# The opening of a fused Fourier and feed-forward kernel: loading the first batch's x chunk by chunk, a third fold buffer, and the first weights issued ahead of a store

## The chip, the cores and the metric

The kernel runs on one NeuronCore of a Trainium2 chip. The metric is device time in microseconds (us) of one execution; less is better. The engines are TensorE (PE), VectorE (DVE), ScalarE (ACT), GpSimd (POOL) and SyncE (SP). SP, ACT and POOL issue the DMAs.

## The reference, cut to what matters

```python
def _attn_ref(x):                       # x: 8 x 3008 x 256
    X = np.fft.fft(x, axis=1)
    X = np.fft.fft(X, axis=2)
    return X.real.astype(np.float32)

def _moe_ref(x, w_in, w_out):           # 24064 x 256, 256 x 2048, 2048 x 256
    h = x @ w_in
    g = h * np.cos(h)
    return (g @ w_out).astype(np.float32)
```

The rows of the first function's result, 8 x 3008 of them, are the tokens of the second.

## The kernel before, in words

**The work.** The sequence transform is split as 3008 = 47 x 64. Its first half (47 points) is a set of matmuls over folded x, its second half (64 points) a set of matmuls with the table `BJ`. The transform along the 256 columns is not done on x at all: it is multiplied into the first weights (`weights`, `keep_weights`: the table `CS` times a 512-column piece of `moe_w_in` gives a piece of `WC` and of `WS`). After that the program is a list of 8 batches x 6 groups x 8 steps, two half steps each, in which PE multiplies (`mm1`, L676, and `mm2`, L767), ACT, DVE and POOL form h * cos(h) between the two, and the groups' results are stored. The transform of batch b + 1 is spread over the steps of batch b. Batch 0 has nothing in front of it, so its transform is an opening of its own, ahead of the first step. The change touches this opening alone.

**The opening.** Batch 0 is loaded as eight chunks of four columns i of x, in the order `parts = (2, 3, 4, 5, 0, 1, 6, 7)`; two neighbouring chunks share one x tile (`xp`). A chunk is four DMAs of `load_x`: direct rows 0 to 31 (128 KB) and 32 to 46 (64 KB) from SP's queue, and the mirrored rows (128 KB and 64 KB, the same rows read backwards in i, in runs of 1 KB) from the queue `other`. For each chunk, `fold` then adds and subtracts columns on DVE (two instructions, L299) and copies two columns on POOL (L306); `first_half` multiplies the folded tile `xf` on PE (L320 to L335) into the PSUM tile `pz`; and ACT copies that to `zs` (L346). Fold tiles come from the pool tag "S" with 3 buffers, of which the opening uses two, by the parity of the chunk number. A fold into a buffer waits until PE has read what stood there.

**The z path.** `store_z(p, 0, 4)` writes the first four of 24 output columns of a pair of chunks (pair p holds chunks 2p and 2p + 1) to a DRAM tile `zd`; `load_z` reads them back transposed as `z`; `second_half(0, 0)` multiplies them with `BJ` into `pb` (L507), from which ACT makes `pq`, the first operand of the steps.

**The weights' path.** `load_cs` loads `CS` (256 KB), `load_w(q)` the q-th piece of `moe_w_in` (512 KB). `weights` is the PE work at L583.

**What sets the order.** The order of instructions on each engine is written out by hand, there is no scheduler. SP executes its DMA issues in program order, waits included. Before: eight issues for chunks 2 and 3 (SP and ACT four each), then `load_x(parts[2], 2, nc.scalar)`, one call of four DMAs for chunks 4 and 5 together, then within the loop the direct rows of chunks 0, 1, 6 and 7 from SP and their mirrored rows from POOL, issued by POOL after its copies of the chunk in hand. Row 32 (`load_row`, L164) goes over POOL too. After the loop: `store_z(1)`, `store_z(2)`, `load_cs`, `load_w(0)`, `store_z(0)` on SP.

**The semaphores of the DMAs.** The DMAs of SP and ACT share eight completion semaphores, taken in turn. An issue that takes a semaphore again waits until the DMA that had it has landed. So at most eight DMAs of these two engines are under way.

**Keeping PE busy.** `keep_busy` issues matmuls on constants (L622) ahead of chunk 2 and behind chunks 2 and 3.

Of the kernel before, what the change touches and what calls it, by code (L numbers as in the profile page):

```python
# [11 lines left out]
FP = mybir.dt.float32  # L12
# [11 lines left out]
IP = 4  # L24
# [105 lines left out]
def kernel(  # L130
# [7 lines left out]
    nc = tc.nc  # L138
# [12 lines left out]
    spool = ctx.enter_context(tc.tile_pool(name="work", bufs=1))  # L151
# [10 lines left out]
    def load_row():  # L162
        for r0, r1, at, by in ((0, 32, 1, 3), (31, 47, 5, 6)):
            nc.gpsimd.dma_start(out=xs[0, 0][at:NX:by, 0:ND], in_=x_r[0, r0:r1, 32, :])  # L164

    def load_x(c, m, other):
        p, q = divmod(c, 2)
        xv = xs[0, p].rearrange("r (i d) -> r i d", d=ND)
        i0, k0 = IP * c, IP * q
        k1 = k0 + IP * m  # L170
        i1 = i0 + IP * m
        skip = 1 if c == 0 else 0
        for r0, r1, at, by in ((0, 32, 0, 3), (31, 47, 2, 6)):
            lo, hi = xv[at:NX:by], xv[at + by // 2 : NX : by]
            nc.sync.dma_start(out=lo[:, k0:k1], in_=x_r[0, r0:r1, i0:i1, :])
            other.dma_start(
                out=hi[:, k0 + skip : k1], in_=x_r[0, r0:r1, 64 - i0 - skip : 64 - i1 : -1, :]
            )
# [55 lines left out]
    def load_cs(eng):  # L234
        eng.dma_start(
            out=CS.rearrange("p (i d) -> p i d", i=2),
            in_=CS_dr.ap().rearrange("(i p) d -> p i d", p=128),
        )

    def load_w(q, eng=nc.sync, i0=0, i1=2):  # L240
        eng.dma_start(
            out=wr[q][:, 512 * i0 : 512 * i1].rearrange("p (i f) -> p i f", f=512),
            in_=moe_w_in[128 * i0 : 128 * i1, 512 * q : 512 * q + 512].rearrange(
                "(i p) f -> p i f", p=128
            ),
        )
# [15 lines left out]
        take_x(0, p)  # L262
    parts = (2, 3, 4, 5, 0, 1, 6, 7)
    for c in parts[:2]:
        load_x(c, 1, nc.scalar)
    WC = cpool.tile([128, NDFF], FP, tag="WC", name="WC")
    WS = cpool.tile([128, NDFF], FP, tag="WS", name="WS")
    wn = cpool.tile([128, 16], FP, tag="wn", name="wn")
# [20 lines left out]
        small.clear()  # L289

    xfs = {}
    xf0 = [spool.tile([128, 2 * IP * 128], FP, tag="S", bufs=3, name="xf") for _ in range(2)]

    def fold(c, e, eng=nc.vector):
        lo = IP * (c % 2)
        xv = xs[0, c // 2].rearrange("r (i d) -> r i d", d=ND)[0:NX, lo : lo + IP]
        xfs[c] = xf0[c % 2]
        fv = xfs[c].rearrange("r (e i d) -> r e i d", e=2, d=128)[0:NX]
        eng.tensor_tensor(  # L299
            out=fv[:, e, :, 1:128],  # L300
            in0=xv[:, :, 1:128],
            in1=xv[:, :, 255:128:-1],
            op=ALU.subtract if e else ALU.add,
        )
        if e:
            nc.gpsimd.tensor_copy(  # L306
                out=fv[:, :, :, 0].rearrange("r e i -> r i e"), in_=xv[:, :, 0:129:128]
            )


    def first_half(c):

        fv = xfs.pop(c).rearrange("r (e c) -> r e c", e=2)[0:NX]
        LE, LO, LE0, LO0, LM = (L[0:NX, 64 * q : 64 * q + 64] for q in range(5))
        pz = psum("pz", "M")
        a = 128 if c == 0 else 0
        for e, (w, w0) in enumerate(((LE, LE0), (LO, LO0))):
            rows = slice(64 * e, 64 * e + 64)
            if a:
                nc.tensor.matmul(  # L320
                    pz[rows, 0:128], lhsT=w0, rhs=fv[:, e, 0:128], start=True, stop=True
                )
            nc.tensor.matmul(
                pz[rows, a:512],
                lhsT=w,
                rhs=fv[:, e, a:512],
                start=not a,
                stop=True,
                skip_group_check=True,
            )  # L330
        if a:
            nc.tensor.matmul(
                pz[64:128, 0:1], lhsT=LE0, rhs=fv[:, 1, 0:1], start=True, stop=True
            )
        nc.tensor.matmul(  # L335
            pz[64:128, a:512:128],
            lhsT=LM,
            rhs=fv[:, 1, a:512:128],
            start=True,
            stop=True,  # L340
        )
        p, q = divmod(c, 2)
        if q == 0:
            tag, n, m = ("xp", 4, XP * ND) if p in (0, 3) else ("zs", 2, 1024)
            zps[p] = spool.tile([128, m], FP, tag=tag, bufs=n, name="zs")
        nc.scalar.copy(out=zps[p][:, 512 * q : 512 * q + 512], in_=pz)  # L346
# [105 lines left out]
    def take_zd(b, half):  # L452
        if (b, half) not in zds:
            zds[b, half] = dpool.tile([32, 2 * NJ * 128], FP, tag="zd", bufs=4, name="zd")
        return zds[b, half]

    def store_z(p, j0=0, j1=NJ, engs=(nc.sync, nc.sync)):
        half, q = divmod(p, 2)
        zd, zs = take_zd(0, half), zps[p][:, 0:1024]
        for e in range(2):  # L460
            p0 = 16 * e + XP * q
            engs[e].dma_start(
                out=zd[p0 : p0 + XP, 256 * j0 : 256 * j1].rearrange("i (y d) -> y i d", d=128),
                in_=zs[64 * e + 2 * j0 : 64 * e + 2 * j1, :].rearrange("y (i d) -> y i d", d=128),
            )
# [155 lines left out]
    def keep_busy(pd, n, start):  # L621
        nc.tensor.matmul(  # L622
            pd[:, 0:n],
            lhsT=VX[:, 0:128],
            rhs=VX[:, 0:n],
            start=start,
            stop=True,
            skip_group_check=True,
        )
# [281 lines left out]
    pds = [psum("pd", tag) for tag in ("H", "H", "M")]  # L911
    for pd in pds:
        keep_busy(pd, 512, True)
    load_x(parts[2], 2, nc.scalar)
    for k, c in enumerate(parts):
        for e in range(2):
            fold(c, e)
        if k == 1:
            load_row()
        if 1 <= k < 5:  # L920
            load_x(parts[3 + k], 1, nc.gpsimd)
        first_half(c)
        for _ in range((1, 2)[k] if k < 2 else 0):
            keep_busy(pds[0], 256, False)
    store_z(1, 0, 4)
    store_z(2, 0, 4)
    load_cs(nc.sync)
    load_w(0)
    store_z(0, 0, 4)
    load_w(1, nc.gpsimd)  # L930
    store_z(3, 0, 4, (nc.sync, nc.scalar))
# [186 lines left out]
```

## Time and profile before

| what | value |
|---|---|
| device time, three runs | 1925.84, 1927.04, 1927.95 us (median 1927.04) |
| profiled execution: device time | 1926.21 us |
| profiled execution: span of the profile | 1924.4 us |
| PE busy over the span | 1914.2 us (99%) |
| DVE, ACT, POOL busy | 1465.8, 1493.0, 1427.7 us |
| DMA moved | 108.64 MB, 56 GB/s on average |
| PE busy from 0 to 30 us, by tens | 8.54, 8.94, 8.78 us |
| PE busy from 120 to 1900 us | 1779.6 of 1780 us |

The profile covers 1924.4 us of the 1926.21 us of its own execution; the other 1.8 us lie around the span. The execution that was profiled lies 0.8 us under the median of the three runs, within their spread of 2.1 us. Times below are in us from the start of the span. The profile gives a matmul whose moving tile has float32 elements as two records.

### The profile page before, as it was taken

The page shows a single profiled execution, that of the slowest core. Times are in us where ns is not written, and L with a number is a line of the kernel's source. Part 1 is how long each engine was busy: PE and PEld are TensorE (multiplying, and loading weights), DVE is VectorE, ACT ScalarE, POOL GpSimd, SP SyncE. Part 2 cuts the span into 40 slices and gives each one's busy share as a digit, 9 for nine tenths or more (in the row PEclk, how much of TensorE's full clock was granted, in tenths as well). Part 3 has the DMA queues.
Part 4 walks back from the last instruction along what each step waited for, and adds up shares of the span by engine and source line. Part 5 has one row for each costly group of instructions (what it writes and reads, how often), then busy time and mean ns, then how long its engine had stood idle before and what let it go on. Part 6 is the DMA issues. An engine that isn't in the chain of part 4 may idle for free.

```text
span 1924.4 us, 29912 instructions
## 1 busy us (share of the span) xinstructions
PE 1914.2 (99%) x9240; PEld 1676.1 (87%) x9240; DVE 1465.8 (76%) x2538; ACT 1493.0 (78%) x3360; POOL 1427.7 (74%) x1705
## 2 busy tenths in 40 slices
PE   9999999999999999999999999999999999999998
PEld 5988899888988889888898888988889888898887
DVE  5777777777777777777777777777777777788787
ACT  3777778778777777778777887778777887778775
POOL 5878758887688776877668786788867788666775
PEclk9999999999999999999999999999999999999999
DMA  8612125011240113311142111511116111100001
GB/s 218 173 24 49 41 54 122 19 42 42 70 102 21 40 44 89 79 34 32 41 116 54 38 24 44 132 36 41 28 39 143 25 41 25 41 22 15 12 15 31
DMA packets 199251, 108.64 MB, mean 56 GB/s; under 512 B 113298, under 2 KB 182640, under 8 KB 198916
## 3 DMA queue, kind: packets, MB, share of 16 engines
q1 hardware_dynamic: 195092, 102.89, 22.7%
q0 software_dynamic: 864, 2.48, 0.4%
q10 hardware_dynamic: 3136, 1.36, 0.3%
q8 instruction: 75, 1.23, 0.3%
q14 instruction: 84, 0.69, 0.1%
HBM read 69.40 MB, written 48.40 MB: 61 GB/s over the span
## 4 chain that ended last, share of the span: by engine, by line
PE 87%; DMA 4%; SPq 4%; POOL 2%; DVE 1%; ACT 1%; issue 1%; DVEq 0%; POOLq 0%
PE M L767 52%; PE H L676 30%; PE pb L507 2%; DMA xp<-in_x_dram 2%; SPq L208 2%; PE pz L397 2%; SPq L905 1%; POOL xf L374 1%; PE pw L583 1%; DMA nb<-nd 1%; SPq L215 1%; DMA xp<-xr 0%; DMA nd<-pq 0%; POOL S L734 0%; PE pd L622 0%
## 5 line engine op out<-in xcount | busy, mean ns | idle before, releaser
L734 POOL TENSOR_TENSOR S<-r 128x512 f32<-128x512 f32 (+1 forms) x383 | 475.5, 1242 | 396.8 <-DVE r L718 344.1
L714 ACT ACTIVATE r<-r 128x512 f32<-128x512 f32 (+1 forms) x768 | 477.0, 621 | 254.8 <-DVE r L708 253.3
L708 DVE SCALAR_TENSOR_TENSOR r<-r,H 128x512 f32<-128x512 f32 (+1 forms) x768 | 519.0, 676 | 195.8 <-ACT r L704 169.0
L767 PE MATMUL M<-S,VX 128*128 128x256 f32 (+1 forms) x2304 | 619.8, 376 | 0.0
L718 DVE SCALAR_TENSOR_TENSOR r<-H,r 128x512 f32<-128x512 f32 (+1 forms) x768 | 519.1, 676 | 127.8 <-ACT r L714 86.7
L767 PEld LDWEIGHTS M<-S,VX 128*128 128x128 f32 x2304 | 435.4, 190 | 71.6 <-issue 22.7
L676 PE MATMUL H<-pq,WC 128*128 128x256 f32 (+1 forms) x1536 | 453.2, 377 | 0.1
L676 PE MATMUL H<-pq,WS 128*128 128x256 f32 (+1 forms) x1536 | 450.9, 375 | 0.0
L704 ACT ACTIVATE r<-H 128x512 f32<-128x512 f32 (+1 forms) x768 | 447.8, 583 | 0.2 <-DVE H L692 0.2
L692 DVE TENSOR_TENSOR H<-ew,H 128x256 f32<-128x256 f32 (+1 forms) x768 | 325.0, 423 | 113.6 <-PE H L676 52.9
L767 PE MATMUL M<-r,w 128*128 128x256 f32 (+1 forms) x1536 | 387.6, 375 | 0.0
L657 ACT ACTIVATE H<-nb,wn 128x256 f32<-128x256 f32 (+1 forms) x766 | 366.2, 478 | 1.8 <-DVE WS L594 0.6
L688 ACT ACTIVATE ew<-H 128x256 f32<-128x256 f32 (+1 forms) x768 | 288.0, 375 | 91.0 <-PE H L676 85.2
L767 PEld LDWEIGHTS M<-r,w 128*128 128x128 f32 x1536 | 300.3, 196 | 27.6 <-issue 0.5
L676 PEld LDWEIGHTS H<-pq,WS 128*128 128x128 f32 x1536 | 290.2, 190 | 34.6 <-issue 2.7
L676 PEld LDWEIGHTS H<-pq,WC 128*128 128x128 f32 x1536 | 279.7, 190 | 44.2 <-ACT H L657 7.7
L740 POOL TENSOR_TENSOR S<-S,r 128x256 f32<-128x256 f32 (+1 forms) x383 | 275.8, 720 | 30.0
L741 POOL TENSOR_TENSOR S<-r,S 128x256 f32<-128x256 f32 (+1 forms) x383 | 275.2, 719 | 30.0
L767 PE MATMUL M<-r,VX 128*128 128x256 f32 (+1 forms) x768 | 225.2, 375 | 0.0
L767 PE MATMUL M<-S,w 128*128 128x256 f32 (+1 forms) x768 | 225.2, 375 | 0.0
L767 PEld LDWEIGHTS M<-S,w 128*128 128x128 f32 x768 | 150.4, 196 | 14.6
L767 PEld LDWEIGHTS M<-r,VX 128*128 128x128 f32 x768 | 145.8, 190 | 14.6
(86 smaller groups left out, 913.5 us busy)
## 6 DMA issues: line engine op xcount, KB each, us to landing
out_dram<-ob SPq DMA_DIRECT2D x724, 32.0 KB
xp<-in_x_dram SPq DMA_DIRECT2D x119, 128.0 KB
xp<-xr SPq DMA_DIRECT2D x112, 128.0 KB
z<-zd SPq DMA_DIRECT2D x28, 384.0 KB
xr<-in_x_dram SPq DMA_DIRECT2D x14, 752.0 KB
zd<-zs SPq DMA_DIRECT2D x98, 96.0 KB
nb<-nd SPq DMA_DIRECT2D x39, 128.0 KB
wr<-in_moe_w_in_dram SPq DMA_DIRECT2D x3, 512.0 KB
```

The source lines that it names most:

```text
L657: nc.scalar.activation(out=h.H[:, 0:T], in_=s.nb[:, 0:T], func=AF.Copy, bias=0.25, scale=wn[:, f : f + 1])
L676: nc.tensor.matmul(h.H[:, 0:T], lhsT=W[:, 128 * f : 128 * f + 128], rhs=s.pq[:, e * T : e * T + T], start=False, stop=True, skip_group_che ...
L688: nc.scalar.mul(out=h.ew[:, 0:T], in_=h.H[:, 0:T], mul=2.0)
L692: nc.vector.tensor_tensor(out=h.H[:, T : 2 * T][:, ::-1], in0=h.ew[:, 0:T], in1=h.H[:, 0:T], op=ALU.subtract)
L704: nc.scalar.activation(out=r, in_=y, func=AF.Copy, bias=BIG, scale=1.0)
L708: nc.vector.scalar_tensor_tensor(out=r, in0=r, scalar=-BIG, in1=y, op0=ALU.add, op1=ALU.subtract)
L714: nc.scalar.activation(out=r, in_=r, func=AF.Sin, bias=0.0, scale=SIN_SCALE)
L718: nc.vector.scalar_tensor_tensor(out=r, in0=y, scalar=-0.25, in1=r, op0=ALU.add, op1=ALU.mult)
L734: tt(out=sv[:, 0:2], in0=qv[:, 1:2].to_broadcast([128, 2, T]), in1=qv[:, 0:4:3], op=ALU.subtract,)
L740: tt(out=sv[:, 2], in0=sv[:, 1], in1=gv[:, 0, 0], op=ALU.subtract)
L741: tt(out=sv[:, 3], in0=gv[:, 1, 0], in1=sv[:, 2], op=ALU.add)
L767: nc.tensor.matmul(acc[key][m // 2][:, 256 * (m % 2) : 256 * (m % 2) + T], lhsT=w, rhs=a, start=first, stop=s.fp == 7, skip_group_check=True,)
```

## The change

`load_x` loses its count of chunks and always loads one. Chunks 4 and 5 become two calls of four DMAs each, both with the mirrored rows on ACT's queue, instead of one call of four DMAs twice the size. The fold buffers become three, taken in turn by the chunk's place in `parts`. `load_cs` and `load_w(0)` move ahead of `store_z(2, 0, 4)` in SP's order.

```diff
-    def load_x(c, m, other):
+    def load_x(c, other):
         p, q = divmod(c, 2)
         xv = xs[0, p].rearrange("r (i d) -> r i d", d=ND)
         i0, k0 = IP * c, IP * q
-        k1 = k0 + IP * m
-        i1 = i0 + IP * m
+        i1, k1 = i0 + IP, k0 + IP
...
     for c in parts[:2]:
-        load_x(c, 1, nc.scalar)
+        load_x(c, nc.scalar)
...
-    xf0 = [spool.tile([128, 2 * IP * 128], FP, tag="S", bufs=3, name="xf") for _ in range(2)]
+    xf0 = [spool.tile([128, 2 * IP * 128], FP, tag="S", bufs=3, name="xf") for _ in range(3)]
...
-        xfs[c] = xf0[c % 2]
+        xfs[c] = xf0[parts.index(c) % 3]
...
-    load_x(parts[2], 2, nc.scalar)
+    for c in parts[2:4]:
+        load_x(c, nc.scalar)
     for k, c in enumerate(parts):
         for e in range(2):
             fold(c, e)
         if k == 1:
             load_row()
         if 1 <= k < 5:
-            load_x(parts[3 + k], 1, nc.gpsimd)
+            load_x(parts[3 + k], nc.gpsimd)
         first_half(c)
...
     store_z(1, 0, 4)
-    store_z(2, 0, 4)
     load_cs(nc.sync)
     load_w(0)
+    store_z(2, 0, 4)
     store_z(0, 0, 4)
```

The built programs differ in this way, engine by engine: SP and ACT have two DMA issues more each. On PE, DVE and POOL no instruction is added, removed or moved; what changes there is which semaphores they wait for (the fold tiles of chunks 4 and 1 have buffers of their own). The eight semaphores are dealt out anew: ACT's four issues for chunks 4 and 5 wait for the landings of the second (64 KB) mirrored load of chunk 2, of the two mirrored loads of chunk 3, and of the first direct load of chunk 4.

## The prediction

> **What bounds the kernel now.** I read the page, then the windows over the first 30 us, then the chain of waits, then the timelines of POOL and DVE. First, the page:
>
> ```profile
> span 1924.4 us, 29912 instructions
> PE 1914.2 (99%) x9240; PEld 1676.1 (87%) x9240; DVE 1465.8 (76%) x2538; ACT 1493.0 (78%) x3360; POOL 1427.7 (74%) x1705
> PE   9999999999999999999999999999999999999998
> ```
>
> PE is idle for 1924.4 - 1914.2 = 10.2 us in all. From 120 to 1900 us the windows give 1779.6 busy of 1780 us. So the steps are PE's own time, which this change leaves alone; all that it can win or lose is the moment at which they start. The opening, by windows (busy us of PE, PEld, DVE, ACT, POOL, then granted clock, DMA share, GB/s):
>
> ```profile
> 9.00:12.00 3.00, 2.15 (x11) 1.14 (x8) 1.01 (x2) 0.59 (x1) 1.60 (x4) 1.00 0.87 221
> 12.00:15.00 3.00, 3.00 (x18) 1.65 (x17) 2.78 (x6) 0.86 (x2) 3.00 (x8) 1.00 0.77 224
> 15.00:18.00 3.00, 3.00 (x19) 1.46 (x17) 3.00 (x6) 1.47 (x3) 1.88 (x4) 1.00 0.58 166
> 18.00:21.00 3.00, 1.78 (x10) 0.86 (x8) 0.59 (x1) 1.18 (x3) 0.74 (x2) 1.00 0.97 309
> 24.00:27.00 3.00, 3.00 (x12) 1.52 (x11) 1.27 (x3) 0.00 (x0) 1.05 (x2) 1.00 0.25 67
> ```
>
> From 9 to 12 us the DMA engines are full and DVE waits. From 15 to 18 us DVE is full, and the DMA engines, at 0.58, have too little asked of them. From 18 to 21 us PE waits and the DMA engines are full again. The chain, in order of time (start, us, what):
>
> ```profile
> 11.00 0.74 POOL xf L306
> ...
> 14.72 0.59 ACT zs L346
> ...
> 15.34 0.26 SPq L462
> ...
> 15.99 0.41 SPq L235
> ...
> 16.45 4.57 DMA wr<-in_moe_w_in_dram
> 21.15 5.40 PE pw L583 x12
> ...
> 27.57 0.49 ACT pq L519
> ```
>
> SP stands at `store_z(2)` until chunk 5's `zs` is copied (15.3), and `CS` and the first weights go out only then; PE has finished the last chunk at 19.8 and waits for the weights until 21.15. A second path ends almost together with it: the last `zs` copy at 20.41, `store_z(3)` landed at 23.48, the last `load_z` at 26.07 (landings are the trace's semaphore records of each DMA), `pb` at 26.4.
>
> What holds the chunks is on POOL:
>
> ```profile
> 11.00 0.73 POOL L306 COPY xf<-xp 96x8 f32<-96x8 f32 x1 [1.40 <-PE pd L622]
> 11.67 1.07 POOL L176 DMA_DIRECT2D xp<-in_x_dram  x2
> 12.74 0.21 POOL L306 COPY xf<-xp 96x8 f32<-96x8 f32 x1
> 12.87 1.06 POOL L176 DMA_DIRECT2D xp<-in_x_dram  x2
> 13.93 0.23 POOL L306 COPY xf<-xp 96x8 f32<-96x8 f32 x1
> 14.10 1.06 POOL L176 DMA_DIRECT2D xp<-in_x_dram  x2
> ```
>
> The first copy is chunk 4's. The profile names PE's `pd` as its releaser, but the last of the four DMAs of chunks 4 and 5 landed at 10.77, and POOL's and DVE's wait for that semaphore ended at 10.79: it was the DMA. From there POOL runs without a pause: copy, two issues (chunk 1), copy, two issues (6), copy, two issues (7). DVE's twelve remaining folds follow from 10.99 to 18.59.
>
> **The change part by part.**
>
> *Chunks 4 and 5 by themselves.* Two issues more on SP (2 x 0.58 us, its median here) and two on ACT (2 x 0.62). SP has spare places; ACT's next work is chunk 2's `zs` at 8.27. ACT's four issues now wait for landings at 4.96, 6.45, 6.64 and chunk 4's first direct load. That one was half of a DMA that landed at 8.96, so I take 7.9. The issues fall at 5.0, 6.5, 7.1 and 8.0; ACT is free at 8.6, which puts `zs` back by 0.3 us, with three further `pz` buffers as cover (without it, PE would wait 0.3 us at chunk 0). Chunk 4's data are complete when ACT's second issue (6.5, 64 KB) lands. Such loads took 2.2 us (POOL, the least) to 3.6 us (ACT beside full engines): 8.7 to 10.1, and I take 9.4, between them, since the engines are still near full there. That is 1.4 us before 10.77. Chunk 5 by the same rows: 8.0 + 2.2 to 3.6, about 10.9.
>
> Whether four DMAs more cost anything by themselves is a rival below. In the trace landings come 0.3 us apart with eight under way: the fixed parts lie beside other transfers, so I add nothing.
>
> *The third buffer.* Chunk 4's fold waits for no PE work; before, chunk 2's was read at 8.2, ahead of 10.77, so this was worth nothing there. Later it takes off DVE's and POOL's waits for `pz`, 0.2 and 0.65 us in the waits. No cost: the pool has three buffers either way, and the first step takes one at 40 us, 20 us after the opening's last use.
>
> *POOL's chain* then starts at 9.6 instead of 11.00. Chunk 5's copy, 1.74 us later (12.74 - 11.00), is due at 11.3, behind its data. Chunk 0's is due at 9.6 + 2.93 = 12.5; its data landed at 12.92, from POOL issues that don't move, beside direct loads that now come later, so 12.3 to 12.9. Chunk 7's second issue moves from 14.64 to 13.3 or 13.7, and its landing (2.2 us later before) from 16.81 to about 15.8.
>
> *DVE.* Twelve folds took 7.6 us without a gap. They start 1.4 us earlier and lose about 0.3 us to waits for chunks 5 and 0: they end at 17.5 instead of 18.59. PE's last chunk ended 1.2 us after DVE (19.78): 18.7. The last `zs`: 19.35 instead of 20.41.
>
> *Weights ahead of the second part's z.* SP now reaches `CS` after sixteen x issues and `store_z(1)`, at about 13.3, and the weights at 13.8 instead of 16.45. `CS`, the weights and the rest of x share the engines: 768 KB at 250 KB per us is 3.1 us behind about 14.8, so the weights land near 18 instead of 21.02, before PE needs them. PE starts L583 at 18.9 instead of 21.15, and its 5.40 us end at 24.3, 2.2 us earlier. The second half of that work needs POOL's 512 KB, issued at 18.00 behind chunk 7's copy and landed at 23.06; with the copy 1 us earlier it lands by 21.5, needed at 22.3. `store_z(2)` is put behind the weights: it lands near 18 instead of 17.6, and nobody reads it before `load_z`, after 21.
>
> *The z path.* `store_z(3)` goes out at 19.35 and took 2.9 us beside the weights' transfers, 2.0 us for `store_z(2)` without them: 21.4 to 22.3. `load_z` took 26.07 - 23.48 = 2.6 us: `pb` at 24.3 to 25.2 instead of 26.4, a gain of 1.2 to 2.1 us. This is now later than PE's own end, so it counts. What follows is a chain of handings-on (the weights' row over DRAM, then pieces 2 and 3, the third landing at 38.23, with PE at its work at 38.29): it moves with the rest only if each earlier DMA does, and the engines are full from 28 us on, so I take the lower half.
>
> **Sum.** 1.5 us less: 1926.2 - 1.5 = 1924.7 us for the profiled execution, and 1927.04 - 1.5 = 1925.5 us for the median, which lay 0.8 us above it. That is 0.08%; a measurement of this kernel can tell about 0.2% (3.85 us) from no change.
>
> **The rivals.**
>
> *Off the path.* The gain is lost at the later hand-over, where piece 3 lands 0.06 us before PE takes it up. For it: the DMA share of 0.79 to 1.03 in the windows from 27 to 42 us. Against it: the share of 0.25 from 24 to 27, so that everything asked for earlier can flow earlier. Time: 1926.6 to 1927.4.
>
> *The eight places bind.* With eight semaphores and half-sized DMAs, less is under way: the least time from issue to landing is 2.2 us here, and four DMAs more, in eight places, put the stream back by 4 x 2.2 / 8 = 1.1 us. Then 0.4 us of the gain is left: 1926.6. Against it: the 0.3 us between landings. The Trainium skill ("DMA: Bandwidth & Descriptors", Anatomy of one DMA) gives each DMA a fixed part of about 2.0 us, an estimate of 1.0 us in the same way.
>
> *Slower, the weights starve the mirrored rows.* `CS` and weights, 768 KB on SP's queue, now meet the mirrored rows of chunks 6 and 7, 384 KB on POOL's queue, of which chunk 7 is the last that DVE needs. With half of 250 KB per us these take 3.1 us from 13.7 and land at 16.8, as before; with a third, 4.6 us: 18.3, 1.5 us behind before. The split decides: under half, the last fold starts after its old 17.3. Price 0 to 1.5 us on the z path: up to 1928.5. Against it: POOL's packets are 4 KB, those of weights and `CS` 2 and 1 KB.
>
> *PE's clock falls back.* A longer gap, while chunk 0's data are waited for, could take the clock down; the first matmuls (L622, 512 columns) follow each other at 0.85 us, twice their later 0.43, until 7.3 us. A second such stretch of 6 us at half speed costs 3 to 6 us: 1930 to 1933. Against it: PE was idle 1.37 us before 21.15 with 1.00 granted after it, and the new order has no longer gap by the sum above. The Trainium skill ("TensorE: Matmul & The Clock Gate", Part 1) puts the idle window at about 3.4 us, which speaks against it too.
>
> *More than summed.* z and weights both arrive at the early ends and the chunks stay full: 2.5 to 4 us less, 1923.0 to 1924.5.
>
> **How the numbers follow.** Forecast (0.5 to 2.5 us less) 0.64; off the path 0.12; places 0.06; starved rows 0.09; clock 0.03; more than summed 0.06. The range leaves out the clock, the ends of the last two and scatter of the three runs (2.1 us wide): 1923.7 to 1928.1. Faster by over 0.2% needs the far end of the last case: 0.04. Slower by over 0.2% needs the clock, or starved rows and a lost hand-over together: 0.05. Within: 0.91.
>
> **What would show it.** In the profile after: chunk 4's fold (DVE L299, third pair) and POOL's copy near 9.6 instead of 11.0; POOL's last x issue near 13.5; the weights' DMA on SP near 13.8; L583 on PE near 18.9 without a DMA ahead of it in the chain; the chain running instead over `zd` and `z` to L507 near 24.8; the next L676 near 26.9 instead of 28.36. Wrong would be: chunk 4 still near 10.8 (the eight places then bound the stream), the last fold after 18.6 (starved rows), L583 early but L676 still at 28.4, or any change in PE's step time after 60 us.

## The result: slower by 4.2 us

| | median | lowest to highest | runs |
|---|---|---|---|
| before | 1926.47 us | 1925.32 to 1929.26 | 22 |
| after | 1930.69 us | 1927.48 to 1932.97 | 22 |

The ratio is 1.0019, with a 95% interval of 1.0013 to 1.0025. The prediction was 1925.5 us, in a range that ended at 1928.1: wrong in its sign. The new times are also wider apart, 5.5 us from lowest to highest, against 3.9. The profiled execution took 1929.98 us, 0.7 us under its own median. A second profile of the same kernel, taken among the experiments, took 1933.06 us. The two lost their time in partly different ways, and both are needed.

### The profile page after: what moved, and what is told of

Read it like the earlier page. It is cut to its first block, busy times and chain, and to the rows that moved or that the text cites. A ratio compares the mean times of both kernels' runs of the same rounds, so it can differ in the third digit from the quotient of the medians.

```text
span 1928.2 us, 29920 instructions
## 1 busy us (share of the span) xinstructions
PE 1916.6 (99%) x9240; PEld 1675.8 (87%) x9240; DVE 1465.5 (76%) x2538; ACT 1493.5 (77%) x3360; POOL 1428.4 (74%) x1705
## 3 DMA queue, kind: packets, MB, share of 16 engines
q0 software_dynamic: 864, 2.48, 0.4%
## 4 chain that ended last, share of the span: by engine, by line
PE 86%; DMA 4%; SPq 4%; POOL 3%; DVE 1%; issue 1%; ACT 0%; ACTq 0%; POOLq 0%; DVEq 0%
PE M L766 52%; PE H L675 30%; DMA xp<-in_x_dram 2%; PE pb L506 2%; PE pz L396 2%; SPq L207 2%; SPq L904 1%; POOL xf L373 1%; DMA xp<-xr 1%; SPq L214 1%; DMA nb<-nd 0%; POOL S L733 0%; DMA wr<-in_moe_w_in_dram 0%; POOL S L739 0%; DVE r L717 0%
## 5 line engine op out<-in xcount | busy, mean ns | idle before, releaser
L766 PE MATMUL M<-S,VX 128*128 128x256 f32 (+1 forms) x2304 | 619.8, 376 | 0.0
L766 PEld LDWEIGHTS M<-S,VX 128*128 128x128 f32 x2304 | 435.4, 190 | 71.6 <-issue 22.7
L675 PE MATMUL H<-pq,WC 128*128 128x256 f32 (+1 forms) x1536 | 453.4, 377 | 0.8 <-ACT H L656 0.7
L675 PE MATMUL H<-pq,WS 128*128 128x256 f32 (+1 forms) x1536 | 451.0, 375 | 0.0
L766 PE MATMUL M<-r,w 128*128 128x256 f32 (+1 forms) x1536 | 387.6, 375 | 0.0
L766 PEld LDWEIGHTS M<-r,w 128*128 128x128 f32 x1536 | 300.2, 196 | 27.7 <-issue 0.5
L675 PEld LDWEIGHTS H<-pq,WS 128*128 128x128 f32 x1536 | 290.1, 190 | 34.9 <-issue 2.7
L675 PEld LDWEIGHTS H<-pq,WC 128*128 128x128 f32 x1536 | 279.6, 190 | 45.5 <-ACT H L656 9.3
L766 PE MATMUL M<-r,VX 128*128 128x256 f32 (+1 forms) x768 | 225.2, 375 | 0.0
L766 PE MATMUL M<-S,w 128*128 128x256 f32 (+1 forms) x768 | 225.2, 375 | 0.0
L766 PEld LDWEIGHTS M<-S,w 128*128 128x128 f32 x768 | 150.3, 196 | 14.6
L766 PEld LDWEIGHTS M<-r,VX 128*128 128x128 f32 x768 | 145.8, 190 | 14.6
```

The source lines that it names most:

```text
L675: nc.tensor.matmul(h.H[:, 0:T], lhsT=W[:, 128 * f : 128 * f + 128], rhs=s.pq[:, e * T : e * T + T], start=False, stop=True, skip_group_che ...
L766: nc.tensor.matmul(acc[key][m // 2][:, 256 * (m % 2) : 256 * (m % 2) + T], lhsT=w, rhs=a, start=first, stop=s.fp == 7, skip_group_check=True,)
```

## The profile after

The first two lines of the page of the changed kernel:

```profile
span 1928.2 us, 29920 instructions
PE 1916.6 (99%) x9240; PEld 1675.8 (87%) x9240; DVE 1465.5 (76%) x2538; ACT 1493.5 (77%) x3360; POOL 1428.4 (74%) x1705
```

The span grew by 3.8 us. By the first H matmul (L675 now; the lines behind `load_x` have moved up by one) the kernel is 1.05 us behind before, by the first M matmul (L766) 2.26 us, by the last 3.18 us, and the last 0.6 us come behind that one. So most of the loss lies ahead of the first M, but not all of it. The windows of the opening show where (busy us of PE, PEld, DVE, ACT, POOL, then granted clock, DMA share, GB/s):

```profile
9.00:12.00 3.00, 2.77 (x13) 1.33 (x10) 1.73 (x3) 0.59 (x1) 2.38 (x5) 1.00 0.81 233
12.00:15.00 3.00, 3.00 (x19) 1.75 (x17) 2.06 (x4) 1.17 (x2) 2.67 (x7) 1.00 0.87 249
15.00:18.00 3.00, 2.63 (x15) 1.22 (x13) 2.56 (x4) 1.01 (x2) 1.25 (x2) 1.00 0.84 269
18.00:21.00 3.00, 1.72 (x8) 0.66 (x6) 1.28 (x2) 0.75 (x2) 1.41 (x2) 1.00 0.35 104
...
39.00:42.00 3.00, 2.18 (x6) 0.97 (x6) 1.70 (x4) 2.32 (x6) 2.37 (x5) 1.00 0.77 240
```

The DMA engines now move 269 GB/s from 15 to 18 us (166 before), as intended; but from 18 to 21 us they have little to do, and PE is as idle there as before (1.72 us busy, 1.78 before). What PE waits for has changed: not the weights but chunk 7. Another hole, not there before, opens after 39 us. The chain of waits (start, us, what) names both:

```profile
13.67 0.49 POOL xp L175
14.16 4.87 DMA xp<-in_x_dram
19.32 0.75 POOL xf L305
20.15 1.58 PE pz L322 x4
21.83 0.60 ACT zs L345
22.44 2.40 DMA zd<-zs
...
29.39 3.62 SPq L461
33.05 0.87 SPq L604
33.95 6.63 DMA wr<-in_moe_w_in_dram
40.63 1.98 PE pw L582 x4
```

POOL asks for chunk 7's second mirrored load (64 KB) at 14.16, and it takes 4.87 us instead of 2.2. The last fold starts at 19.32 instead of 17.32. Further on SP stands 3.62 us in issuing one `z` store (2.92 before), so the second weights' row `wn` goes out at 33.05 and the fourth weight piece at 33.95. The row landed at 39.33 (36.97 before), and it is what PE waits for first, by way of ACT:

```profile
39.35 0.45 ACT L656 ACTIVATE H<-nb,wn 128x225 f32<-128x225 f32 x1 [1.40 <-DMA wn<-wd]
39.86 0.65 PE L675 MATMUL H<-pq,WC 128*128 128x225 f32 x2 [0.69 <-ACT H L656]
```

The fourth piece landed at 40.59, just ahead of PE's L582 at 40.63, where before it landed 0.06 us in time.

In the second profile chunk 7's mirrored rows landed at 20.66 (issued at 14.94), and something more happened. Its windows, from the end of chunk 6 on:

```profile
18.00:21.00 3.00, 1.64 (x6) 0.64 (x6) 0.51 (x2) 1.11 (x2) 0.05 (x1) 1.00 0.60 198
21.00:21.50 0.50, 0.00 (x0) 0.00 (x0) 0.50 (x1) 0.00 (x0) 0.50 (x1) 1.00 0.00 0
21.50:22.00 0.50, 0.22 (x1) 0.25 (x2) 0.50 (x2) 0.00 (x0) 0.50 (x2) 0.64 0.00 0
...
24.00:27.00 3.00, 3.00 (x6) 1.41 (x5) 0.00 (x0) 0.59 (x1) 0.00 (x0) 0.50 0.50 155
...
28.00:28.50 0.50, 0.50 (x2) 0.21 (x1) 0.38 (x1) 0.00 (x0) 0.00 (x0) 0.53 0.35 101
28.50:30.00 1.50, 1.50 (x5) 0.68 (x4) 0.59 (x2) 0.00 (x0) 0.00 (x0) 1.00 0.34 99
```

And PE's timeline there:

```profile
21.78 2.48 PE L322 MATMUL pz<-xf,L 96*64 96x512 f32 x4 [2.13 <-POOL xf L305]
24.05 0.32 PE L334 MATMUL pz<-xf,L 96*64 96x4 f32 x2
24.30 7.47 PE L582 MATMUL pw<-wr,CS 128*128 128x512 f32 x12
```

PE waited 2.13 us for chunk 7, and the granted clock fell to 0.50. The mean of 0.64 over the half microsecond puts the fall at 21.64, that of 0.53 the rise at 28.47: 6.83 us at half speed. The twelve L582 matmuls took 7.47 us instead of 5.42. The page's slices, 48 us each, show nothing of it.

## The experiments

All medians below stand beside runs of the kernel before on the same chip (1926.6 to 1927.1 us). With five rounds the interval of a ratio is about 0.0009 to either side, 1.7 us; differences under that are read from the traces only, and from single profiles.

### Which part of the change costs

*The change with the old order: `store_z(2)` back ahead of `CS` and the weights.*

```diff
+    store_z(2, 0, 4)
     load_cs(nc.sync)
     load_w(0)
-    store_z(2, 0, 4)
```

> The whole change except for the order on SP: store_z(2) stands ahead of CS and the first weights again. Theory S (the early weights starve the mirrored rows of chunks 6 and 7): chunk 7's last mirrored load lands at 15.5 to 16.8 us instead of 19.0, the weights go out near 15 us, L582 starts on PE near 20 instead of 21.7, and the time is 1 us below before, 1925 to 1926. Theory P (eight places, or more DMAs, put the stream of x back): chunk 7 lands late here too, near 18 to 19, and the time is 1929 to 1931. Theory H (any shift upsets the later hand-over of the third weight piece): the opening is earlier, but PE waits 2 us near 39 us and the time is 1928 to 1930.

Measured: 1928.67 us, ratio 1.0009 (1.0000 to 1.0018). Chunk 7's mirrored rows landed at 17.29, the last fold started at 17.58. In this profile the first H came at 27.77, 0.59 us earlier than before, but the first M at 43.63, 0.96 us later: PE waited 1.04 us at 38.56, behind the same row `wn`. The opening's gain was there, and was lost at the hand-over. The order's part of the change is thus some 2 us, and it is the part that makes chunk 7 late; another 2 us stay.

*The order alone, in the kernel before.*

```diff
-    store_z(2, 0, 4)
     load_cs(nc.sync)
     load_w(0)
+    store_z(2, 0, 4)
```

> The kernel before with nothing but the new order on SP: CS and the first weights ahead of store_z(2). Theory S: the weights go out near 13 us, chunk 7's mirrored loads land near 19 instead of 16.8, L583 starts near 21.5 or later, and the time is 1929 to 1931, as after the whole change. Theory P: the splitting is the cause, so the order alone is worth 0 to 1 us less: 1925.5 to 1926.5. Theory H: slower by 2 us if the opening moves at all in either direction, 1928 to 1930.

Measured: 1931.22 us, ratio 1.0022 (1.0013 to 1.0031): as much as the whole change. POOL's timeline:

```profile
14.00 1.05 POOL L176 DMA_DIRECT2D xp<-in_x_dram  x2
16.42 0.62 POOL L306 COPY xf<-xp 96x8 f32<-96x8 f32 x1 [1.37 <-DMA CS<-dft_CS]
20.13 1.32 POOL L306 COPY xf<-xp 96x8 f32<-96x8 f32 x2 [3.09 <-DMA zd<-zs]
```

The two copies at 20.13 are those of chunks 6 and 7, one behind the other: both chunks were held up. The releaser that the profile names, a store of `z` that landed at 20.14, is not what POOL's copy reads; by the landings, chunk 6's mirrored rows came at 19.94 and chunk 7's at 20.35, to either side of that store. In this profile too the granted clock fell to half, from 20.94 to 27.77, behind a wait of 2.17 us.

*The third fold buffer alone.*

```diff
-for _ in range(2)]
+for _ in range(3)]
...
-        xfs[c] = xf0[c % 2]
+        xfs[c] = xf0[parts.index(c) % 3]
```

> The kernel before with three fold buffers and nothing else. All theories: the folds of chunks 4 and 5 still wait for the joint load at 10.8 us, so nothing moves by more than 0.3 us: 1926 to 1927. A difference of more than 1 us would say that the buffers matter by themselves.

Measured: 1926.74 us, ratio 1.0001 (0.9992 to 1.0010). No difference can be told.

*Chunks 4 and 5 by themselves alone.*

```diff
-    load_x(parts[2], 2, nc.scalar)
+    for c in parts[2:4]:
+        load_x(c, 1, nc.scalar)
```

> The kernel before with chunks 4 and 5 loaded by two calls of four DMAs each, two fold buffers, the old order on SP. Theory S: chunk 4's fold starts near 10.3 us as it does after the change, chunk 7 lands near 16, the time is 0.5 to 1 us below before: 1925.5 to 1926. Theory P: 1929 to 1931, chunk 7 late. Theory H: 1928 to 1930 with a PE wait near 39 us.

Measured: 1928.98 us, ratio 1.0010 (1.0001 to 1.0018). Chunk 4's fold started at 11.07 (10.99 before), the last fold at 18.23, and PE waited 0.96 us at 39.35 behind the row `wn`; the fourth weight piece landed at 40.08. The first H came 0.28 us later than before, the first M 1.75 us. So the split brings nothing for chunk 4 in this profile, and costs about 2 us. The order alone costs 4.45 us by the medians and the split 2.2, the whole change 4.2: the parts do not add up, and on top of the split the order costs 2.0 to 2.3. The clock, below, may be part of the reason.

### The weights against the mirrored rows

*`CS` alone moved ahead of `store_z(2)`; the weights stay behind it.*

```diff
-    store_z(2, 0, 4)
     load_cs(nc.sync)
+    store_z(2, 0, 4)
     load_w(0)
```

> The kernel before with only CS (256 KB) ahead of store_z(2); the weights (512 KB) stay behind it. CS and weights together, 768 KB, cost 4.4 us as a change of their own. Theory S (early weights starve the mirrored rows of chunks 6 and 7): a third of the bytes, and CS has passed before chunk 7's rows are due: chunk 7 lands at 17 to 18 us and the time is 0 to 1.5 us above before, 1926.5 to 1928. Theory W (the late store_z(2) is the cause, whatever stands ahead of it): it is behind CS here too, and the time is 1929 or more.

Measured: 1927.81 us, ratio 1.0006 (0.9997 to 1.0015); chunk 7's mirrored rows at 18.35. A quarter of the order's cost, with a third of its 768 KB.

*The order alone, with the mirrored rows asked for earlier.* POOL issues those of chunks 0 and 1 together, and those of chunks 6 and 7 one chunk sooner than before.

```diff
-        if 1 <= k < 5:
-            load_x(parts[3 + k], 1, nc.gpsimd)
+        for c1 in ((), parts[4:6], parts[6:7], parts[7:8])[k] if k < 4 else ():
+            load_x(c1, 1, nc.gpsimd)
```

> The kernel before with the new order on SP (CS and weights ahead of store_z(2), 1931.2 by itself), and POOL's mirrored loads one chunk earlier: chunks 0 and 1 after chunk 3's copy, 6 after chunk 4's, 7 after chunk 5's. Theory S: chunk 7's rows are asked for at 13 to 14 us, ahead of the weights' packets, land by 17.5, PE has the weights when it ends chunk 7, and the time falls back to 1926 to 1928. Theory W: chunk 7 lands early, but the time stays at 1930 or more.

Measured: 1927.41 us, ratio 1.0002 (0.9994 to 1.0011): of the order's 4.45 us, 3.8 are gone, with every transfer and the order on SP as in the order alone. POOL's timeline and the chain:

```profile
12.61 1.06 POOL L176 DMA_DIRECT2D xp<-in_x_dram  x2
18.88 0.62 POOL L306 COPY xf<-xp 96x8 f32<-96x8 f32 x1 [2.27 <-DMA zd<-zs]
```

```profile
18.88 0.63 POOL xf L306
19.51 0.08 issue
19.59 1.58 PE pz L323 x4
```

Chunk 7's rows are asked for 1.4 us sooner and land at 18.59; they still take 5.4 us, but chunk 6 is not held up, and PE's wait is 1.25 us, with the clock at 1.00 throughout.

*The same edit in the changed kernel.*

```diff
-            load_x(parts[3 + k], nc.gpsimd)
+        for c1 in ((), parts[4:6], parts[6:7], parts[7:8])[k] if k < 4 else ():
+            load_x(c1, nc.gpsimd)
```

> The whole change, with POOL's mirrored loads one chunk earlier. Theory S: 2 to 4 us below the whole change, 1926.5 to 1928.5; what is left above before is the split of chunks 4 and 5 (1 to 2 us). If starvation is not the cause: 1930 to 1931.

Measured: 1928.45 us, ratio 1.0007 (0.9998 to 1.0016): 2.2 us under the changed kernel.

*The same edit in the kernel before, as a control.*

> The kernel before with POOL's mirrored loads one chunk earlier and nothing else: the control for the two runs above. DVE is full from 11 to 18.6 us, so chunks that land earlier bring at most 0.3 us: 1926 to 1927. More than 1 us below before would say that the earlier loads gain by themselves, and that the two runs above can't be read as starvation alone.

Measured: 1926.46 us, ratio 0.9998 (0.9989 to 1.0007). Where no weights are in the way, asking earlier is worth nothing. So most of what the order costs is the meeting of the two transfers.

### What the split costs

*Only the direct rows of chunks 4 and 5 split (SP)*, in the kernel before; here and in the next run `load_x` takes counts of its own for direct and mirrored rows.

```diff
-    load_x(parts[2], 2, nc.scalar)
+    load_x(parts[2], 1, nc.scalar, 2)
+    load_x(parts[3], 1, nc.scalar, 0)
```

> The kernel before, with only SP's direct rows of chunks 4 and 5 in two calls (two issues more on SP); ACT's mirrored rows stay joint. The whole split alone cost 2.2 us, with the four z stores behind the second weight piece landing 9.3 us after their issue instead of 7.9 and the fourth weight piece at 40.1 instead of 38.2. Theory Q (the place in SP's own queue: two issues more on SP change how the later descriptors fall): the first of these stores takes 9.3 us here, PE waits for the fourth piece, time 1928 to 1929.5. Theory L (only the full split, four DMAs more, turns the eight semaphores by half): 7.9 us and 1926 to 1927. Theory A (ACT's later issues are the cause): 7.9 us, 1926 to 1927.

Measured: 1927.18 us, ratio 1.0004 (0.9995 to 1.0013).

*Only the mirrored rows split (ACT).*

```diff
-    load_x(parts[2], 2, nc.scalar)
+    load_x(parts[2], 2, nc.scalar, 1)
+    load_x(parts[3], 0, nc.scalar, 1)
```

> The kernel before, with only ACT's mirrored rows of chunks 4 and 5 in two calls; SP's queue is as before. Theory Q: the first z store behind the second weight piece takes 7.9 us, no wait for the fourth piece, 1926 to 1927. Theory A: 9.3 us and 1928 to 1929.5. Theory L: 7.9 us, 1926 to 1927.

Measured: 1927.60 us, ratio 1.0006 (0.9997 to 1.0015). Each half is under what this can resolve (0.55 and 0.97 us by the medians); together they make 1.5 us of the split's 1.9 to 2.2.

*The changed kernel with the fourth weight piece and the second weights' row asked for ahead of the stores of `z`.*

```diff
+    load_w(3)
+    load_wn(1)
     for p in (1, 2):
         store_z(p, 4)
-    load_wn(1)
-    load_w(3)
```

> The changed kernel, with the fourth weight piece and the second weights' row ahead of the four z stores (pairs 1 and 2) on SP. Theory T (two costs: 1.0 us in the opening from the starved mirrored rows, some 2.7 us from the later hand-over of the fourth piece): the fourth piece lands by 35 us, PE has no wait near 39 us, and the time falls by 2 to 3 us to 1927.5 to 1928.5; what is left above before is the opening's 1 us. If the loss were all in the opening (one cost), 1930 to 1931 as before this edit.

Measured: 1931.81 us, ratio 1.0026 (1.0016 to 1.0036). From the first H to the first M matmul it took 14.3 us, as in before (15.5 in the changed kernel): the hole at 39 us is closed. But the profiled execution, 1928.18 us, is the fastest of the nine, and the median is no better. By their granted clocks (0.998 or less, see "The clock") the clock fell in five of the nine; the other four took 1928.18 to 1931.61 us.

*The same with the old order.*

> Chunked loads and three fold buffers, the old order of the first weights (as in the run with the old order), and the fourth weight piece ahead of the four z stores. Theory T: the opening's 0.6 us earlier first step is kept, no wait near 39 us: 1925.5 to 1926.3, below before. If the opening's gain does not reach the steps: 1926.5 to 1927.5; if moving the stores back makes the z of the later groups late, PE waits at L507 near 57 us and it is 1928 or more.

Measured: 1928.03 us, ratio 1.0008 (0.9999 to 1.0017): 0.6 us under the old order without it, less than can be told.

*The same move in the kernel before, as a control.*

> The kernel before with only this: the fourth piece of the weights and the next weights' row asked for ahead of the stores of z's first two pairs. Control for e7 and e8: before does not wait for that piece (it lands at 38.23, PE takes it up at 38.29), so if the late hand-over is a symptom of a late opening the time stays at before's, 1926 to 1927.2; if the move itself costs something (the stores then land later and are read later), 1927.5 to 1929.

Measured: 1926.57 us, ratio 0.9998 (0.9989 to 1.0007). The move costs nothing that can be told. So no gain from the move is shown: the late row and fourth piece, plain as they stand in the first profile, give back 0.6 us with the old order and nothing in the changed kernel's median, with an interval of some 1.7 us around each.

*The split, with the mirrored rows of chunks 4 and 5 from POOL, where they take none of the eight semaphores.*

```diff
-    load_x(parts[2], 2, nc.scalar)
+    for c in parts[2:4]:
+        load_x(c, 1, nc.gpsimd)
```

> The kernel before, with chunks 4 and 5 loaded one by one (as in the change), but their mirrored rows from GpSimd's queue, ahead of the loop, where no completion semaphore of SP and ACT is taken; order and buffers as before. Places theory (the split costs 2 us because four DMAs more in eight places put the stream of x back): without the places the stream is not put back, so chunk 4's fold starts by 10.3, chunk 5 is complete by about 11, chunk 7's mirrored rows land by 16.8, the last fold starts by 17.4 and the time is that of before or up to 0.8 us less, 1926 to 1927. Rival (smaller DMAs, or a late fourth piece of the weights, cost the 2 us wherever they are issued from): last fold after 17.8, 1928 to 1929.

Measured: 1929.35 us, ratio 1.0013 (1.0004 to 1.0021). Chunks 4 and 5 came as early as hoped (folds at 9.89 and 11.09), yet chunk 7's rows landed at 18.13 and the last fold started at 18.43. The stream ends later without the places as well, so they are not shown to hold it. But the first chunk's fold also began at 6.92 instead of 5.16, since these rows were asked for from 2.0 us on, beside those of chunks 2 and 3. So this run does not say by itself what the split costs and why.

*The same, with the third buffer and the fourth piece first.*

> The same loads as in e16, with the three fold buffers and with the fourth piece of the weights and the next weights' row asked for ahead of the stores of z's first two pairs. It takes what each theory calls free and leaves out the order of the change. If places and the late fourth piece are the two costs of the split: first step's first M near 41.5 to 42.2, 1925.5 to 1926.5, at most 1.2 us under before. If the opening is bound elsewhere: 1927 to 1929.

Measured: 1932.66 us, ratio 1.0022 (1.0012 to 1.0032), three of eight runs at 1928.1 to 1928.8, five at 1932.3 to 1933.7. A clear miss, and of the profile it is the clock that shows why:

```profile
6.00:9.00 3.00, 1.21 (x3) 0.19 (x2) 1.22 (x3) 0.00 (x0) 0.76 (x2) 1.00 0.78 192
...
12.00:15.00 3.00, 3.00 (x10) 1.63 (x6) 1.74 (x4) 0.59 (x1) 3.00 (x8) 0.50 0.83 253
15.00:18.00 3.00, 3.00 (x10) 0.98 (x10) 0.65 (x2) 0.31 (x1) 0.91 (x3) 0.50 0.55 172
```

PE waited 1.79 us for its first chunk, and the clock stood at half from 9.90 to 20.14 us; chunk 7, complete at 18.2, found PE far behind. The other kernels' profiles show 1.00 there. The five slow runs have a mean granted clock of 0.995 or 0.996, the three fast ones 0.999 or 1.000.

### The clock

*The changed kernel once more, for a second profile.*

> The changed kernel once more, for a second profile of its opening. If the starved mirrored rows are its rule and not a draw: chunk 7's mirrored rows land after 18.3, the last fold starts after 18.6, first M after 44, and the time is 1929 to 1932. If the first profile was a bad draw: chunk 7 by 17.5, first M near 42.5, 1927 to 1928.

Measured: 1933.06 us; its lines stand above. Late rows are the rule with this order: in its six profiles with POOL's issues as they were (the changed kernel twice, the order alone, the fourth piece first and the two below) chunk 7's mirrored rows landed between 18.87 and 20.66. In the eight profiles with the old order and these rows from POOL as before they landed between 16.39 and 17.58, and at 18.13 and 18.18 in the two just told, where the stream had been put in another order.

How often the clock falls can be read from the mean granted clock over the span, which stands on record for every run. It is 0.999 in all profiled executions without a fall, 0.998 in the two with 6.83 us at half speed, and 0.996 with all three edits (13.65 us in all). A single fall of 3.41 us can hide in the rounding. Of the 22 runs of the changed kernel ten have 0.997 or 0.998, with a median of 1931.76 us; the other twelve have a median of 1929.84 us. With the order alone it is ten runs of eleven, with the order and the rows asked for earlier one of eleven, and 5 of the 142 runs of the kernel before that stand beside the experiments. So the clock falls in about half of the changed kernel's executions, and where it does not, the change still costs 3.4 us.

*The changed kernel with PE kept busy behind chunk 6.* Three matmuls on constants, 1.5 us in the profile, in PE's wait for chunk 7.

```diff
-        for _ in range((1, 2)[k] if k < 2 else 0):
+        for _ in range({0: 1, 1: 2, 6: 3}.get(k, 0)):
             keep_busy(pds[0], 256, False)
```

> The changed kernel with one thing more: behind chunk 6 PE gets three matmuls on constants (256 columns, 0.43 us each, 1.3 us together), which fill most of its wait for chunk 7 and feed nothing. Theory C (clock): in many executions of the changed kernel the late chunk 7 leaves PE idle for about 2 us, the granted clock falls to 0.50 for 6.8 us (as in the second profile) and this costs up to 3.4 us, which is the upper half of its times. Then the runs above 1931 go away, the median falls by 1.5 to 2.5 us to 1928.2 to 1929.2, and the profile shows 1.00 throughout. Theory S alone (late rows, the clock rarely matters): the wait for chunk 7 ends no earlier, so the median stays at 1930.2 to 1931.2, with runs up to 1933.

Measured: 1931.00 us, ratio 1.0019 (1.0010 to 1.0028), from 1929.01 to 1933.06. The profiled execution took 1929.88 us. PE's timeline:

```profile
20.28 1.56 PE L621 MATMUL pd<-VX 128*128 128x256 f32 x6
21.77 1.37 PE L322 MATMUL pz<-xf,L 96*64 96x512 f32 x4
22.98 0.23 PE L334 MATMUL pz<-xf,L 96*64 96x4 f32 x2
23.13 5.42 PE L582 MATMUL pw<-wr,CS 128*128 128x512 f32 x12
```

Chunk 7's rows landed at 20.44, as late as in the second profile, and PE took chunk 7 at the same 21.77; but the clock stayed at 1.00, the four L322 matmuls took 1.37 us instead of 2.48, and the first H matmul came at 30.86 instead of 33.58. In this pair of profiles the clock is worth 2.7 us at that point and 3.2 us in the time. The median did not fall, though. One run of the eleven has a granted clock under 0.999 (0.997, at 1933.06 us); the other ten took 1929.01 to 1932.96 us. So the clock was held in nearly all of them, and the slower ones are slow without it: the theory that the late rows alone set the time was right, and the theory of the clock missed by 2 us. The added work is not free either. In this profile the last fold began at 20.73, and PE took up chunk 7 0.83 us behind that fold in the two profiles without the work, so by this estimate it could have started at 21.56 instead of 21.77.

*The order alone with PE kept busy behind chunk 1*, ahead of the wait in which its clock fell (four such matmuls).

> The kernel of e2 (the order alone) with four such matmuls (1.7 us) behind chunk 1, ahead of the 2.2 us for which PE waited there before its clock fell in e2's profile. Theory C: the rows of chunks 6 and 7 still land near 20, but PE works them off at full clock: first M near 45 instead of 48.1, median 1928 to 1929 instead of 1931.2. Theory S alone: 1930.5 to 1932, first M near 48.

Measured: 1930.07 us, ratio 1.0015 (1.0007 to 1.0024), 1.1 us under the order alone, between the two expectations; the intervals overlap. One of its eleven runs has a granted clock under 0.999, against ten of eleven for the order alone. In its profile (1929.83 us) chunk 7's rows landed at 20.35, to the hundredth as in the order alone, the clock stayed at 1.00, and the first H matmul came at 30.92 instead of 33.78.

The three groups of profiles side by side:

| kernel | chunk 7's mirrored rows landed | lowest clock, 8 to 50 us | first H | first M | this execution |
|---|---|---|---|---|---|
| before | 16.81 | 1.00 | 28.36 | 42.67 | 1926.21 |
| after | 19.03 | 1.00 | 29.41 | 44.93 | 1929.98 |
| after, PE kept busy | 20.44 | 1.00 | 30.86 | 45.18 | 1929.88 |
| order alone, PE kept busy | 20.35 | 1.00 | 30.92 | 46.09 | 1929.83 |
| order alone | 20.35 | 0.50 | 33.78 | 48.10 | 1932.35 |
| after, again | 20.66 | 0.50 | 33.58 | 47.89 | 1933.06 |

Late rows without the clock: 3.6 to 3.8 us more than before in these executions, of which 1.05, 2.50 and 2.56 us stand at the first H; the rest comes behind it. With the clock: 6.1 to 6.9 us. These are single executions: by the runs, the two groups of the changed kernel are 1.9 us apart.

## Why the prediction was wrong, point by point

*What bounds the kernel* held in the main: PE's own time is the steps', and the change moved the moment at which they start. But "any change in PE's step time after 60 us", a sign of being wrong, came in a small way: PE lost 0.19 us near 315 us and 0.35 us near 1811 us (times of the kernel before). Both stand in all ten profiles of kernels that split direct and mirrored rows, the first alone in the two that split one of them, and neither in the eight without a split. So 0.5 us of the split's cost lies far behind the opening; why is open.

*Weights ahead of the second part's z*: the issue was right (13.95, forecast 13.8), what it does was not. The weights landed at 20.32, not near 18. L582 started at 21.72 and, in the second profile, at 24.30, not at 18.9, and not for want of weights: PE had to go through chunk 7 first.

*POOL's chain* is the step that failed. Its end, "its landing (2.2 us later before) from 16.81 to about 15.8", took the 2.2 us of the old order over into a stretch where 768 KB had been put beside it. The runs showed 4.9 us (after) and 5.7 (again): 19.03 and 20.66. With it fell *DVE* (the last folds began at 19.32 and 20.95, for an end of 17.5; a start after 18.6 was the prediction's own sign of starved rows) and *the z path* (`pb` at 27.47 and 31.60 for 24.3 to 25.2).

*The rival of the starved mirrored rows* was the right mechanism, with its place and its point of decision, and it was mis-sized and given 0.09. Its price went down to a third of the engines for POOL's rows, and no further. In the records of packets, from 17 to 18 us of the first profile, POOL's queue had 14 packets of 187 ns each and the weights 124 of 89 ns: 2.6 of the 16 us that 16 engines have in 1 us, or 16%. Before, with nothing large beside them, 43 to 47 such packets went through in each us from 13 to 16. "Against it: POOL's packets are 4 KB" was no protection at all. And the slack was judged by bytes over a mean rate, where the last packet counts: in the second profile the weights' DMA and the last mirrored rows ended 0.11 us apart, at 20.77 and 20.66.

*PE's clock falls back*, given 0.03, was the other one, at chunk 7 and not at chunk 0. Its size was near: 6.83 us at half speed for "6 us", 2.7 us measured at the first H matmul for "3 to 6". What spoke against it did not hold: the new order did have longer gaps, 2.13 and 2.17 us where the clock fell. The Trainium skill ("TensorE: Matmul & The Clock Gate", Part 1), which says that the half rate comes after an idle window of about 3.4 us, was taken to mean that a shorter wait is safe; in these two profiles it was not. The clock falls in about half of the changed kernel's executions, so it is a part of the loss beside the starved rows, not the whole.

*Chunks 4 and 5 by themselves* was the term with the largest gain (1.4 us): the folds of chunk 4 started at 10.27 and 11.09 in the two profiles, for 9.6 and against 10.99 before. Over the eight profiles with both halves split and the mirrored rows on ACT's queue the mean is 10.5, over the eight without a split 11.0: a gain of 0.5 us. The estimate read a single DMA's duration off a row, where the engines were full already. That smaller pieces moved the order in which they land and not the rate is a likely reading, which no run isolates. The rival of *the eight places* (0.06) named a later stream; the run that took the places away had one as well, so they were not shown to be the cause.

*The third buffer* at nothing was right. *The hand-over* was a rival only as a lost gain (*off the path*), by piece 3. In the first profile it took 1.2 us more from H to M than before, in that of the old order 1.55 us, and there it cost the whole gain of the opening and more. PE's wait was mostly for the row `wn`. By the controls, asking for both earlier gains no more than the noise.

Three things stay open: why the split costs 1.5 to 2 us, of which the profiles show waits at the hand-over and 0.5 us far behind it, but no cause; why the changed kernel's slower executions without a fall of the clock are slow; and why POOL's rows get so small a share. None of the versions beat the kernel before by more than the noise.

## What to carry to other kernels

A load that is moved ahead competes with everything that is in flight at its new place: find the last transfer there that somebody waits for, and price it at the share that a small queue really gets beside a large one, not at its old duration. If both are wanted, ask for the small and urgent one first; here one chunk earlier on POOL gave back 3.8 of 4.45 us. And add to any wait on PE of about 2 us the price of its clock, here about 2 us by the runs and near 3 in one pair of profiles, which comes in some executions only; look for it in windows of a microsecond and in the granted clock of every run, since the page's slices hide it.

## What the runs showed of the hardware

- The granted clock fell to half after waits on PE of 2.13 and 2.17 us, and in the run with all three edits after 1.79 and 1.88 us; after waits of 1.86 and 1.87 us in two other profiles it did not. The stretches at half speed lasted 6.83, 6.83, 10.24 and 3.41 us: 2, 2, 3 and 1 times 3.41. The stretches at full speed ahead of them, 17.07, 13.65, 3.41 and 6.83 us, are whole multiples too. So the clock is decided on a grid of 3.41 us, the length that the Trainium skill gives for its window in the same Part 1. The grid lies elsewhere in each execution: the first stretch at full speed began at 7.31 us in the profile before, at 4.57 us in the second one after. The window need not be idle throughout: in the 3.41 us ahead of the four falls PE had been busy for 1.42, 1.25, 1.62 and 1.53 us. In every other window of the grid at full speed, over all twenty profiles up to 30 us from the end, it was busy for 2.03 us or more. So in these runs the limit lies between 1.62 and 2.03 of 3.41 us, and a half, 1.71 us, would fit. A wait's place on the grid then explains why equal waits end differently.
- Beside 768 KB on SP's queue, loads of 128 and 64 KB on POOL's queue took 4.7 to 6.3 us instead of 2.2 to 2.5 (chunk 7's two, in the changed kernel, its second profile and the two kept-busy runs, against before). From 17 to 18 us of the first profile 14 of POOL's 4 KB records went through beside 151 of `CS` and weights. The Trainium skill ("DMA: Bandwidth & Descriptors", Queues, rings and completion order) has each DMA engine take turns between queues, packet by packet, where a packet is typically some 9 to 17 descriptors. No run here tells how many of the profile's records make up such a packet, so 14 beside 151 neither bears this out nor speaks against it.
- The first of the four `z` stores behind the third weight piece took, from issue to landing, 7.7 to 8.0 us in some profiles and 8.9 to 9.4 in others, with the split and without it. SP stands in the fourth one's issue meanwhile, 3.62 us in the changed kernel's chain and 2.92 us before, and the second weights' row and the fourth weight piece wait behind it. What decides between the two is open.
